# Attention output products one stretch earlier, and the column sums of w1 in f32r, in a fused attention and mixer kernel

## The chip, the cores and the metric

The kernel runs on one core of a Trainium2 chip. The metric is the device time of one execution in microseconds. The engines named here are PE (matrix products, with PEld for the loading of their weights), DVE and ACT (element-wise work; ACT does the exponentials), POOL (element-wise work on SBUF) and SP (here only a queue that issues DMAs).

## The reference

x is 2048 x 448. There are 16 heads of 28 columns that share one key and one value head. The outputs of attention and of a small mixer are weighed by a gate:

```python
q = (x @ wq).reshape(B, S, H, Dh).transpose(0, 2, 1, 3)
k = x @ wk
v = x @ wv
p = softmax(einsum("bhqd,bkd->bhqk", q, k) * Dh ** -0.5)
a = einsum("bhqk,bkd->bhqd", p, v).transpose(0, 2, 1, 3).reshape(B, S, H * Dh) @ wo
h = gelu(layernorm(x) @ w1)
x1 = x + concatenate(shifts of h's four column groups) @ w2
b = x1 + gelu(layernorm(x1) @ w3) @ w4
g = sigmoid((x * gate_w).sum(-1))
out = g * a + (1 - g) * b
```

## The kernel before

**Precision.** Most products are made in f32r: an operand is split into a high part (rounded to f32r) and a low part (what is left), and two or three products of the parts are added in PSUM. The products of values and of wo are plain f32.

**Stage 1 (to about 120 us).** Queries, keys, values and the gate are made by `stage_q`, four groups of heads for each of four blocks of 512 tokens, and go through DRAM. Between them stand the statistics of the first layer norm, and w1 is centred so that the norm's mean need not be subtracted: `sum_w1` adds the four row chunks of w1 on POOL to wsum, `centre_w1` sums wsum over the partitions by a product with a matrix of ones (line 396), and DVE subtracts the mean from w1. Then come the products with w1 and w2.

**Stage 2 (to about 400 us).** The products with w3 and w4, block by block.

**Stage 3 (to the end).** Attention in 16 units u, four blocks of 512 queries times four groups of four heads. A unit has 8 stretches v of two tiles of 128 keys; k = 8u + v counts the stretches. In a stretch stand, in this order:

- the scores of two key tiles (line 909): for each tile 12 products on PE into four banks, one for each head. The four heads use four row groups of PE side by side.
- for each tile, ACT's exponentials of heads 0, 1 and 2 from PSUM into p (line 942), and DVE's copy of head 3 into pd (line 939). There are 8 banks of PSUM, taken in turn by scores, products and values, and given back to the end of the row by whoever read them out. ACT makes the exponentials of both copies of pd at the end (line 947).
- in k = 3 to 10 one of eight late products with w4 (`w4_half`).
- from unit 1 on one half of an output product (`wo_half`, line 823): 128 tokens of an earlier unit by 224 columns of wo, evicted by DVE to ot (line 814). A unit has 8 halves, i = 0 to 7. In the last unit, two stand in each of the stretches 4 to 6, and two in the tail behind the loop.
- the values of the stretch before (line 952), in two halves of 256 queries, on four column groups of PE; DVE adds each half to o (line 956; a copy, line 967, where a unit begins).

The row sums of the softmax come out of the values' products as a column of ones. A unit is normalised in the next unit: in stretch 0 SP sends the sums as rt (`sums_begin`, line 789); in stretch 1 DVE checks them and makes reciprocals (`recip`, lines 785 and 796), and SP sends these to DRAM (rd, line 798) and back to all partitions (rb, line 800); in stretch 3 DVE multiplies o by rb to on (`norm`, line 805), which the half products of that unit read.

Every engine works through its instructions in the order in which the program lists them. For the attention loop that is the text of the loop.

Of the kernel before, what the change touches and what calls it, by code (L numbers as in the profile page):

```python
# [9 lines left out]
F32 = mybir.dt.float32  # L10
F32R = mybir.dt.float32r
AF = mybir.ActivationFunctionType
ALU = mybir.AluOpType
# [3 lines left out]
P = 128  # L17
S = 2048
D = 448
# [18 lines left out]
def f32(ap):  # L38
    return ap.bitcast(F32)
# [3 lines left out]
def gated_mix_kernel(  # L43
# [12 lines left out]
    nc = tc.nc  # L56
# [31 lines left out]
    def misc_tile(name):  # L88
        return psA.tile([P, 512], F32, tag="misc", bufs=1, name=name)
# [103 lines left out]
    NU = NB * NG  # L193
# [56 lines left out]
    with tc.tile_pool(name="s1b", bufs=1) as s1b, \  # L250
            tc.tile_pool(name="ps1", bufs=1, space=PSUM) as ps1:
        s1_stack = ExitStack()
        s1 = s1_stack.enter_context(tc.tile_pool(name="s1", bufs=1))
# [128 lines left out]
            rb_of[b] = s1.tile([P, 512], F32, tag="rsb", bufs=2, name=f"rsb_{b}")  # L382
            nc.sync.dma_start(rb_of[b][0:C], rd.rearrange("(o t) p -> o (t p)", o=1).broadcast_to([C, 512]))

        ones = s1.tile([P, P], F32, name="ones")
        nc.gpsimd.memset(ones, 1.0)
        wsum = s1.tile([P, 512], F32, tag="hf", bufs=3, name="wsum")[:, 0:D]

        def sum_w1():
            nc.gpsimd.tensor_tensor(wsum, w1raw[:, 0, :], w1raw[:, 1, :], ALU.add)  # L390
            nc.gpsimd.tensor_tensor(wsum, wsum, w1raw[:, 2, :], ALU.add)
            nc.gpsimd.tensor_tensor(wsum[0:64], wsum[0:64], w1raw[0:64, 3, :], ALU.add)

        def centre_w1():
            ps = misc_tile("wsum_ps")[:, 0:D]
            nc.tensor.matmul(ps, ones, wsum, start=True, stop=True)
            for c in range(4):
                nc.vector.scalar_tensor_tensor(w1raw[:, c, :], ps, -1.0 / D, w1raw[:, c, :],
                                               op0=ALU.mult, op1=ALU.add)
# [237 lines left out]
    with tc.tile_pool(name="s2", bufs=1, reuse_waits="tile") as s2, \  # L637
# [42 lines left out]
        for b in range(NB):  # L680
            acc = [ps2.tile([P, 512], F32, tag="acc", bufs=4, name=f"acc_{b}_{t}") for t in range(4)]
            gs = {}
            for f in range(NF):
# [35 lines left out]
                u = M_AT.get(b * NF + f)  # L719
# [32 lines left out]
    with tc.tile_pool(name="s3", bufs=1, reuse_waits="tile") as s3, \  # L752
# [7 lines left out]
        def take():  # L760
            return banks.pop(0)

        def bank(name):
            ps = banks.pop(0)
            banks.append(ps)
            return ps

        def q_fetch(u):
            if u < NU:
                q_load(u, s3.tile([P, 512], F32, tag="qr", bufs=1, name=f"qr_{u}"))  # L770

        def q_begin(u):
            q_split(u, s3.tile([P, 512], F32R, tag="qh", bufs=3, name=f"qh_{u}"),
                    s3.tile([P, 512], F32R, tag="ql", bufs=3, name=f"ql_{u}"), nc.gpsimd)
# [12 lines left out]
        def sums_begin(u, o):  # L787
            rt = s3.tile([P, 16], F32, tag="rt", bufs=2, name=f"rt_{u}")
            nc.sync.dma_start(rt, o[0:128:32, :].rearrange("j (a b) -> j a b", b=16))
            return u, o, rt  # L790
# [12 lines left out]
        def norm(u, o, rb):  # L803
            on_of[u] = s3.tile([P, 512], F32, tag="on", bufs=2, name=f"on_{u}")
            nc.vector.tensor_mul(on_of[u], o, rb)
# [11 lines left out]
        def wo_job(u, t, cols=slice(0, D), evict=by_one, queue=nc.sync, then=None):  # L817
            b, g = divmod(u, NG)
            n = 4 * b + t
            ps = take()  # L820
            for j in range(4):
                tok = slice(t * P + 32 * j, t * P + 32 * j + 32)
                nc.tensor.matmul(ps[32 * j:32 * j + 32, cols], on_of[u][:, tok], wof[:, g, cols],  # L823
                                 start=True, stop=True, tile_position=(0, 32 * j))
            if g == 0 and cols.start == 0:
                ot_of[n] = s3.tile([P, D], F32, tag="ot", bufs=5, name=f"ot_{n}")
            before = x1[:, n, cols] if g == 0 else ot_of[n][:, cols]
            def finish():
                evict(n, ps, before, cols)
                if g == NG - 1 and cols.stop == D:  # L830
                    queue.dma_start(out[0, n * P:(n + 1) * P, :], ot_of[n])
                banks.append(ps)

            if then is None:
                finish()
            else:
                then.append(finish)

        def wo_half(u, i, then=None):
            t, h = divmod(i, 2)  # L840
            wo_job(u, t, slice(224 * h, 224 * h + 224), then=then)
# [3 lines left out]
        def w4_half(i):  # L845
            t, h = divmod(i, 2)
            n = NT - 4 + t
            cols = slice(224 * h, 224 * h + 224)
            tok = slice(t * P, (t + 1) * P)
            gh, gl = last_g  # L850
            ps = bank(f"job_{n}_{h}")[:, cols]
            nc.tensor.matmul(ps, gh[:, tok], w4h[-1][:, 1, cols], start=True, stop=False)
            nc.tensor.matmul(ps, gh[:, tok], w4l[-1][:, 1, cols], start=False, stop=False)
            nc.tensor.matmul(ps, gl[:, tok], w4h[-1][:, 1, cols], start=False, stop=True)
            nc.vector.scalar_tensor_tensor(x1[:, n, cols], ps, gi[:, n:n + 1], x1[:, n, cols],
                                           op0=ALU.mult, op1=ALU.add)
# [44 lines left out]
        p_of, pd_of, o_of, sums, norms = {}, {}, {}, [], []  # L901
        NV = 8

        def scores(u, kt):
            bs = [take() for j in range(4)]
            for i in range(3):
                for j in range(4):
                    for _, _, w, a in score(u, bs[j], j, slice(kt * P, (kt + 1) * P), i=i):
                        nc.tensor.matmul(bs[j], w, a, start=(i == 0), stop=(i == 2), tile_position=(32 * j, 0))  # L909
            return bs  # L910
# [21 lines left out]
        def exps(u, kt, bs):  # L932
            ps = p_of[u, kt] = {}
            for j in READ:
                if j == DRAIN:
                    if kt % 2 == 0:
                        pd_of[u, kt // 2] = turn_of(pd_free)
                    ps[j] = pd_of[u, kt // 2][:, kt % 2, :]
                    nc.vector.tensor_copy(ps[j], bs[j])  # L939
                else:  # L940
                    ps[j] = turn_of(p_free)
                    behind[kt % 2] = nc.scalar.activation(ps[j], bs[j], AF.Exp, scale=SCALE)  # L942
                banks.append(bs[j])

        def late_exps(u, v):
            pd = pd_of.pop((u, v))
            ins = nc.scalar.activation(pd, pd, AF.Exp, scale=SCALE)  # L947
            tc.add_manual_dep(ins.ins, behind[0].ins.name, SYNC, reason="one wait of ACT for its own writes per stretch")

        def value(u, kt, q, pv):  # L950
            for j in range(4):
                nc.tensor.matmul(pv[32 * j:32 * j + 32, q], vext[:, kt, :], p_of[u, kt][j][:, q],  # L952
                                 start=(kt % 2 == 0), stop=(kt % 2 == 1), tile_position=(0, 32 * j))

        def add_value(u, q, pv):
            nc.vector.tensor_add(o_of[u][:, q], o_of[u][:, q], pv[:, q])  # L956
            banks.append(pv)

        def values(u, v):
            if v == 0:  # L960
                o_of[u] = s3.tile([P, 512], F32, tag="o", bufs=2, name=f"o_{u}")
            for q in HALVES:
                pv = take()
                for kt in (2 * v, 2 * v + 1):
                    value(u, kt, q, pv)
                if v == 0:
                    nc.vector.tensor_copy(o_of[u][:, q], pv[:, q])
                    banks.append(pv)
                else:
                    add_value(u, q, pv)  # L970
# [5 lines left out]
        W4_AT = 3  # L976

        for k in range(NU * NV - 1):
            u, v = divmod(k, NV)
            if k == 3:  # L980
                q_begin(1)
                q_fetch(2)
            if v == 6 and u + 2 < NU:
                q_begin(u + 2)
                q_fetch(u + 3)
            for kt in (2 * v, 2 * v + 1):
                exps(u, kt, scores(u, kt))
            late_exps(u, v)
            if 0 <= k - W4_AT < 8:
                w4_half(k - W4_AT)  # L990
            if v >= 4 and u:
                wo_half(u - 1, v - 4)
            if v < 4 and u > 1:
                wo_half(u - 2, v + 4)
            if v >= 4 and u == NU - 1:
                wo_half(u - 1, v)
            if k:
                values(*divmod(k - 1, NV))
            if u and v == 0:
                sums.append(sums_begin(u - 1, o_of[u - 1]))  # L1000
            if u and v == 1:
                norms.append(recip(*sums.pop()))
            if u and v == 3:
                norm(*norms.pop())
        assert not sums and not norms

        u, v = NU - 1, NV - 1
# [37 lines left out]
            value(u, NT - 2, q, pvs[i])  # L1045
        value(u, NT - 1, HALVES[0], pvs[0])
        add_value(u, HALVES[0], pvs[0])
        wo_half(u - 1, 3)
        later = []
        wo_half(u - 1, 7, later)  # L1050
        held = [tail_sums(0)]
# [80 lines left out]
```

## Time and profile before

| | |
|---|---|
| median of 3 runs | 918.75 us (917.4 to 918.87) |
| the profiled execution's own time | 918.12 us |
| its span, first to last instruction | 916.2 us |
| busy in it: PE, ACT, DVE, POOL | 907.5, 634.6, 542.8, 105.3 us |
| exponentials of ACT from PSUM, line 942 | 762, mean 619 ns |
| half products, line 823 | 992 instructions, mean 370 ns |
| products of values, line 952 | 4096 instructions, mean 379 ns |
| granted clock of PE | 0.999 |

A row of a timeline gives the start, the duration, the engine, line and operation, what is written and read, and how many instructions were merged. In brackets stands how long the engine was idle before it, and what ended that. Durations of PE overlap, since the next product enters while the last drains: the distance of two starts is what a product costs. An instruction of DVE may be shown to start shortly before the last one ends.

### The profile page before, as it was taken

The page shows a single profiled execution, that of the slowest core. Times are in us where ns is not written, and L with a number is a line of the kernel's source. Part 1 is how long each engine was busy: PE and PEld are TensorE (multiplying, and loading weights), DVE is VectorE, ACT ScalarE, POOL GpSimd, SP SyncE. Part 2 cuts the span into 40 slices and gives each one's busy share as a digit, 9 for nine tenths or more (in the row PEclk, how much of TensorE's full clock was granted, in tenths as well). Part 3 has the DMA queues.
Part 4 walks back from the last instruction along what each step waited for, and adds up shares of the span by engine and source line. Part 5 has one row for each costly group of instructions (what it writes and reads, how often), then busy time and mean ns, then how long its engine had stood idle before and what let it go on. Part 6 is the DMA issues. An engine that isn't in the chain of part 4 may idle for free.

```text
span 916.2 us, 24001 instructions
## 1 busy us (share of the span) xinstructions
PE 907.5 (99%) x10040; PEld 644.0 (70%) x10040; DVE 542.8 (59%) x1082; ACT 634.6 (69%) x1135; POOL 105.3 (11%) x136
## 2 busy tenths in 40 slices
PE   9999999999999999999999999999999999999997
PEld 7788888888888888875655565556656565556653
DVE  4674264631435736446666666676666666666765
ACT  5542255322232231259999999999999999999995
POOL 2243200212000430031000000000000000000000
PEclk9999999999999999999999999999999999999999
DMA  9822543220222132110000001100011000010001
GB/s 303 306 63 45 163 137 125 39 67 21 41 61 58 24 100 62 38 53 25 25 23 6 27 14 49 32 26 26 3 45 47 26 3 26 22 50 12 15 14 44
DMA packets 41809, 51.81 MB, mean 57 GB/s; under 512 B 9313, under 2 KB 27553, under 8 KB 41697
## 3 DMA queue, kind: packets, MB, share of 16 engines
q1 hardware_dynamic: 38528, 44.54, 16.5%
q10 hardware_dynamic: 3168, 5.70, 1.8%
q8 instruction: 80, 1.31, 0.6%
q14 instruction: 33, 0.26, 0.1%
HBM read 37.04 MB, written 11.93 MB: 53 GB/s over the span
## 4 chain that ended last, share of the span: by engine, by line
PE 97%; ACT 1%; DMA 0%; DVE 0%; issue 0%; ACTq 0%; DVEq 0%
PE bank L952 24%; PE bank L909 22%; PE bank L823 7%; PE acc L677 5%; PE acc L676 5%; PE acc L678 5%; PE g L132 4%; PE g L131 4%; PE g L133 4%; PE hs L455 1%; PE hs L456 1%; PE g L135 1%; PE g L134 1%; PE h L131 1%; PE h L132 1%; PE h L133 1%
## 5 line engine op out<-in xcount | busy, mean ns | idle before, releaser
L942 ACT ACTIVATE p<-bank 128x512 f32<-128x512 f32 x762 | 387.1, 619 | 4.4 <-PE bank L909 3.9
L952 PE MATMUL bank<-p,vext 128*32 128x256 f32 x3080 | 243.9, 379 | 0.8 <-ACT p L942 0.8
L952 PE MATMUL bank<-pd,vext 128*32 128x256 f32 x1016 | 240.3, 379 | 0.0
L939 DVE COPY pd<-bank 128x512 f32<-128x512 f32 x254 | 175.2, 691 | 52.8 <-PE bank L909 51.8
L952 PEld LDWEIGHTS bank<-p,vext 128*32 128x32 f32 x3080 | 125.1, 110 | 83.1 <-ACT p L942 2.1
L666 ACT ACTIVATE gh<-g 128x512 fp32r<-128x512 f32 x55 | 32.8, 597 | 187.4 <-PE g L135 187.4
L956 DVE TENSOR_TENSOR o<-o,bank 128x256 f32<-128x256 f32 x224 | 94.3, 421 | 94.5 <-ACT p L942 50.0
L947 ACT ACTIVATE pd<-pd 128x1024 f32<-128x1024 f32 x127 | 141.1, 1111 | 0.0
L909 PE MATMUL bank<-qh,kH 30*128 30x512 f32 x1024 | 119.0, 443 | 0.0
L668 DVE TENSOR_TENSOR gl<-gf,gh 128x512 fp32r<-128x512 f32 x55 | 37.9, 689 | 124.6 <-ACT gf L667 124.5
L952 PEld LDWEIGHTS bank<-pd,vext 128*32 128x32 f32 x1016 | 110.7, 110 | 0.0
L909 PE MATMUL bank<-ql,kH 28*128 28x512 f32 x1024 | 104.7, 390 | 0.0
L909 PE MATMUL bank<-qh,kL 28*128 28x512 f32 x1024 | 104.5, 391 | 0.0
L909 PEld LDWEIGHTS bank<-qh,kH 30*128 30x128 f32 x1024 | 60.8, 182 | 58.2 <-ACT p L942 47.0
L677 PE MATMUL acc<-w4l,gh 128*128 128x448 f32 x220 | 80.4, 366 | 0.0
L676 PE MATMUL acc<-w4h,gh 128*128 128x448 f32 x220 | 80.3, 365 | 0.0
L678 PE MATMUL acc<-w4h,gl 128*128 128x448 f32 x220 | 80.2, 364 | 0.0
L823 PE MATMUL bank<-wof,on 128*32 128x224 f32 (+1 forms) x992 | 72.9, 370 | 0.3 <-ACT p L942 0.3
L132 PE MATMUL g<-al,w3h 128*128 128x512 f32 x168 | 65.8, 392 | 0.0
L131 PE MATMUL g<-ah,w3h 128*128 128x512 f32 x168 | 65.6, 391 | 0.0
L133 PE MATMUL g<-ah,w3l 128*128 128x512 f32 x168 | 65.5, 390 | 0.0
L909 PEld LDWEIGHTS bank<-ql,kH 28*128 28x128 f32 x1024 | 51.6, 185 | 9.0
(193 smaller groups left out, 1164.1 us busy)
## 6 DMA issues: line engine op xcount, KB each, us to landing
qd<-qf ACTq DMA_DIRECT2D x16, 256.0 KB
qm<-qd SPq DMA_DIRECT2D x16, 256.0 KB
qr<-qd SPq DMA_DIRECT2D x16, 256.0 KB
rb<-rd SPq DMA_DIRECT2D x15, 256.0 KB
x<-in_x_dram SPq DMA_DIRECT2D x4, 896.0 KB
xd<-xt SPq DMA_DIRECT2D x16, 224.0 KB
w34raw<-in_w_dram SPq DMA_DIRECT2D x7, 512.0 KB
w34raw<-in_w_dram SPq DMA_DIRECT2D x7, 448.0 KB
```

What stands on the lines that cost most here:

```text
L131: nc.tensor.matmul(ps, wh[:, c, :], ah[:, c, :], start=(c == 0), stop=False)
L132: nc.tensor.matmul(ps, wh[:, c, :], al[:, c, :], start=False, stop=False)
L133: nc.tensor.matmul(ps, wl[:, c, :], ah[:, c, :], start=False, stop=False)
L676: nc.tensor.matmul(ps, gh[:, tok], w4h[i][:, k, :], start=(f == 0), stop=False)
L677: nc.tensor.matmul(ps, gh[:, tok], w4l[i][:, k, :], start=False, stop=False)
L678: nc.tensor.matmul(ps, gl[:, tok], w4h[i][:, k, :], start=False, stop=(f == stop))
L823: nc.tensor.matmul(ps[32 * j:32 * j + 32, cols], on_of[u][:, tok], wof[:, g, cols], start=True, stop=True, tile_position=(0, 32 * j))
L909: nc.tensor.matmul(bs[j], w, a, start=(i == 0), stop=(i == 2), tile_position=(32 * j, 0))
L939: nc.vector.tensor_copy(ps[j], bs[j])
L942: behind[kt % 2] = nc.scalar.activation(ps[j], bs[j], AF.Exp, scale=SCALE)
L947: ins = nc.scalar.activation(pd, pd, AF.Exp, scale=SCALE)
L952: nc.tensor.matmul(pv[32 * j:32 * j + 32, q], vext[:, kt, :], p_of[u, kt][j][:, q], start=(kt % 2 == 0), stop=(kt % 2 == 1), tile_position ...
```

## The change

In a stretch of the loop the reciprocals (stretch 1) and the normalisation (stretch 3) move ahead of the half products and values, directly behind the copies and exponentials. The half products of a unit move up by one stretch: i = 0 stands at the end of stretch 3, behind the values; i = 1 to 4 in stretches 4 to 7; i = 5 to 7 in stretches 0 to 2 of the next unit. In the last unit, unit 14's halves stand as 0 in stretch 3, (1, 2), (3, 4) and 5 in stretches 4 to 6, and 6 and 7 in the tail.

The sum of w1 is split by POOL into wsh and wsl, both f32r, and the product with ones becomes two f32r products.

```diff
-        ones = s1.tile([P, P], F32, name="ones")
-        nc.gpsimd.memset(ones, 1.0)
+        ones = s1.tile([P, P], F32R, name="ones")
+        nc.gpsimd.memset(f32(ones), 1.0)
         wsum = s1.tile([P, 512], F32, tag="hf", bufs=3, name="wsum")[:, 0:D]
+        wsh = s1.tile([P, 512], F32R, tag="hf", bufs=3, name="wsh")[:, 0:D]
+        wsl = s1.tile([P, 512], F32R, tag="hf", bufs=3, name="wsl")[:, 0:D]
 
         def sum_w1():
...
             nc.gpsimd.tensor_tensor(wsum[0:64], wsum[0:64], w1raw[0:64, 3, :], ALU.add)
+            nc.gpsimd.tensor_copy(wsh, wsum)
+            nc.gpsimd.tensor_tensor(wsl, wsum, f32(wsh), ALU.subtract)
 
         def centre_w1():
             ps = misc_tile("wsum_ps")[:, 0:D]
-            nc.tensor.matmul(ps, ones, wsum, start=True, stop=True)
+            nc.tensor.matmul(ps, ones, wsh, start=True, stop=False)
+            nc.tensor.matmul(ps, ones, wsl, start=False, stop=True)
...
             late_exps(u, v)
-            if 0 <= k - W4_AT < 8:
-                w4_half(k - W4_AT)
-            if v >= 4 and u:
-                wo_half(u - 1, v - 4)
-            if v < 4 and u > 1:
-                wo_half(u - 2, v + 4)
-            if v >= 4 and u == NU - 1:
-                wo_half(u - 1, v)
-            if k:
-                values(*divmod(k - 1, NV))
-            if u and v == 0:
-                sums.append(sums_begin(u - 1, o_of[u - 1]))
             if u and v == 1:
                 norms.append(recip(*sums.pop()))
             if u and v == 3:
                 norm(*norms.pop())
+            if 0 <= k - W4_AT < 8:
+                w4_half(k - W4_AT)
+            if v < 3 and u > 1:
+                wo_half(u - 2, v + 5)
+            if v > 3 and u:
+                for i in (v - 3,) if u < NU - 1 else ((1, 2), (3, 4), (5,))[v - 4]:
+                    wo_half(u - 1, i)
+            if k:
+                values(*divmod(k - 1, NV))
+            if v == 3 and u:
+                wo_half(u - 1, 0)
+            if u and v == 0:
+                sums.append(sums_begin(u - 1, o_of[u - 1]))
...
-        wo_half(u - 1, 3)
+        wo_half(u - 1, 6)
         later = []
         wo_half(u - 1, 7, later)
```

How the instructions of DVE stand in unit 1, stretch 1, before (the copies of head 3, a product of w4, the values into o, check and reciprocal):

```order
L939 COPY pd_3535<-bank_3506 128x512
L939 COPY pd_3535<-bank_3502 128x512
L855 SCALAR_TENSOR_TENSOR x_72<-bank_3503,gi,x_72 128x224
L967 COPY o_4058<-bank_3506 128x256
L967 COPY o_4058<-bank_3508 128x256
L785 SCALAR_TENSOR_TENSOR good<-rt_4019,good 128x16
L796 RECIPROCAL rr_4078<-rt_4019 128x16
```

The same stretch and stretch 3 in the changed kernel (the lines are 5 higher):

```order
L944 COPY pd_3540<-bank_3511 128x512
L944 COPY pd_3540<-bank_3507 128x512
L790 SCALAR_TENSOR_TENSOR good<-rt_4024,good 128x16
L801 RECIPROCAL rr_4060<-rt_4024 128x16
L860 SCALAR_TENSOR_TENSOR x_72<-bank_3508,gi,x_72 128x224
L972 COPY o_4070<-bank_3511 128x256
L972 COPY o_4070<-bank_3513 128x256
```

```order
L944 COPY pd_3542<-bank_3508 128x512
L944 COPY pd_3542<-bank_3512 128x512
L810 TENSOR_TENSOR on_4177<-o_3612,rb_4064 128x512
L961 TENSOR_TENSOR o_4070<-o_4070,bank_3507 128x256
L961 TENSOR_TENSOR o_4070<-o_4070,bank_3508 128x256
L819 SCALAR_TENSOR_TENSOR ot_4201<-bank_3510,gg,x_72 128x224
```

Check and reciprocal moved ahead of three evictions; the normalisation, which stood behind both additions of stretch 3, moved ahead of them, and a half product's eviction (L819) came to the end of that stretch.

PE at the end of that stretch 3 (k = 11), before: the last values are followed by the scores of stretch 4.

```order
L952 MATMUL bank_3503<-p_3527,vext 32x256
L952 MATMUL bank_3503<-p_3528,vext 32x256
L952 MATMUL bank_3503<-pd_3536,vext 32x256
L909 MATMUL bank_3505<-qh_3677,kH 128x512
L909 MATMUL bank_3508<-qh_3677,kH 128x512
```

In the changed kernel, the first half product (four products on column tiles) stands between them:

```order
L957 MATMUL bank_3508<-p_3532,vext 32x256
L957 MATMUL bank_3508<-p_3533,vext 32x256
L957 MATMUL bank_3508<-pd_3541,vext 32x256
L828 MATMUL bank_3510<-wof,on_4177 32x224 x4
L914 MATMUL bank_3513<-qh_3682,kH 128x512
L914 MATMUL bank_3511<-qh_3682,kH 128x512
```

Before, the first half product of unit 0 stood in stretch 4, ahead of its values.

## The prediction

> **What bounds the kernel now.** I read the page first (busy time of each engine, then the chain of work that ended last), then the timelines of PE, ACT, DVE and SP over a few stretches of the attention loop, then the DMA share in short windows.
>
> ```profile
> PE 907.5 (99%) x10040; PEld 644.0 (70%) x10040; DVE 542.8 (59%) x1082; ACT 634.6 (69%) x1135; POOL 105.3 (11%) x136
> PE 97%; ACT 1%; DMA 0%; DVE 0%; issue 0%; ACTq 0%; DVEq 0%
> ```
>
> PE is busy 907.5 of 916.2 us, and 97% of the chain is PE. So only a shorter PE program, or fewer waits in it, shortens the run. The attention loop fills the second half of the span; here is one of its stretches in the timeline of PE (start, duration):
>
> ```profile
> 564.11 0.51 PE L909 MATMUL bank<-qh,kH 30*128 30x512 f32 x4
> ...
> 565.76 0.59 PE L823 MATMUL bank<-wof,on 128*32 128x224 f32 x8
> 566.16 0.39 PE L952 MATMUL bank<-p,vext 128*32 128x256 f32 x3
> ...
> 567.67 0.39 PE L952 MATMUL bank<-p,vext 128*32 128x256 f32 x3
> ...
> 568.00 0.51 PE L909 MATMUL bank<-qh,kH 30*128 30x512 f32 x4
> ```
>
> Scores take 564.11 to 565.76 (1.65 us), one half of an output product 0.40, the values 566.16 to 568.00 (1.84): 3.89 us. The reader should see that nothing stands empty between them. ACT is close behind. At the head of the loop, where PE has less to do, ACT sets its own pace:
>
> ```profile
> 408.31 3.10 ACT L942 ACTIVATE p<-bank 128x512 f32<-128x512 f32 x6
> ...
> 412.12 3.16 ACT L942 ACTIVATE p<-bank 128x512 f32<-128x512 f32 x6
> ```
>
> That is 412.12 - 408.31 = 3.81 us a stretch. So a stretch costs the larger of PE's sum and 3.81: a stretch with one half product is PE's by 0.08 us, one with none is ACT's, and one with two is PE's alone. The rows of PE at the two ends of the loop show the other two kinds:
>
> ```profile
> 447.42 0.51 PE L909 MATMUL bank<-qh,kH 30*128 30x512 f32 x4
> ...
> 449.06 0.42 PE L952 MATMUL bank<-p,vext 128*32 128x256 f32 x3
> ...
> 450.92 0.50 PE L909 MATMUL bank<-qh,kH 30*128 30x512 f32 x4
> ...
> 452.93 0.59 PE L823 MATMUL bank<-wof,on 128*32 128x224 f32 x8 [0.32 <-ACT p L942]
> ...
> 455.18 0.51 PE L909 MATMUL bank<-qh,kH 30*128 30x512 f32 x4
> ```
>
> ```profile
> 895.53 0.51 PE L909 MATMUL bank<-qh,kH 30*128 30x512 f32 x4
> ...
> 897.17 0.96 PE L823 MATMUL bank<-wof,on 128*32 128x224 f32 x16
> ...
> 899.79 0.51 PE L909 MATMUL bank<-qh,kH 30*128 30x512 f32 x4
> ```
>
> The first set is stretch 3 of unit 1 (k = 11), the only one late in the loop with neither a half product nor a product of w4. PE passes it in 450.92 - 447.42 = 3.50 us, and in the next stretch it waits 0.32 us for ACT, so that one takes 4.26. The second set is stretch 6 of the last unit: two half products, 4.26 us, ACT waiting.
>
> **The change, part by part.**
>
> *Half products one stretch earlier.* A unit still has eight of them, one a stretch. What differs is the ends of the loop. The first now falls into k = 11, and the last unit's stretch 6 has one instead of two (the tail keeps two). k = 11 and 12 together took 455.18 - 447.42 = 7.76 us and will take 2 x 3.89 = 7.78: +0.02, since the free PE time there was lost again to ACT. Stretch 6 goes from 4.26 to 3.89: -0.37. Bounds: the new product in k = 11 costs at least nothing and at most its own 0.40; the one removed saves at least nothing and at most 0.40.
>
> *Stretch 3: the product behind the values.* In all 15 units from u = 1 on, scores are followed by values, and the product comes last. From the start of a stretch to the first group behind the scores it is 1.65 us where that is a product (565.76) and 1.64 where it is a value (449.06 - 447.42), so the entry costs the same. The exit from values to scores is 568.00 - 567.67 = 0.33 us, a group every (567.67 - 566.16)/7 = 0.216, so 0.11 is the change of kind; no row shows an exit from a product to scores. I bound it by 0.11 us less and 0.11 more per unit, 1.7 us each way over 15 units, and take nothing, since both are groups of four products on the same four column tiles.
>
> *Reciprocal behind the copies of stretch 1, normalisation behind those of stretch 3.* These are DVE instructions that can now hold up what is queued behind them: the eviction of the half product and the two additions of the values, and through them the banks of the next scores. DVE's rows of unit 5, stretches 1 and 3:
>
> ```profile
> 565.21 1.39 DVE L939 COPY pd<-bank 128x512 f32<-128x512 f32 x2 [0.49 <-PE bank L909]
> 566.51 0.44 DVE L814 SCALAR_TENSOR_TENSOR ot<-bank,gg,ot 128x224 f32<-128x224 f32 x1
> 567.28 0.42 DVE L967 COPY o<-bank 128x256 f32<-128x256 f32 x1 [0.32 <-PE bank L952]
> 568.21 0.42 DVE L967 COPY o<-bank 128x256 f32<-128x256 f32 x1 [0.51 <-ACT p L942]
> 568.55 0.17 DVE L785 SCALAR_TENSOR_TENSOR good<-rt,good 128x16 f32<-128x16 f32 x1
> ...
> 573.00 1.40 DVE L939 COPY pd<-bank 128x512 f32<-128x512 f32 x2 [0.49 <-PE bank L909]
> ...
> 575.06 0.42 DVE L956 TENSOR_TENSOR o<-o,bank 128x256 f32<-128x256 f32 x1 [0.31 <-PE bank L952]
> 575.98 0.42 DVE L956 TENSOR_TENSOR o<-o,bank 128x256 f32<-128x256 f32 x1 [0.50 <-ACT p L942]
> 576.32 0.68 DVE L805 TENSOR_TENSOR on<-o,rb 128x512 f32<-128x512 f32 x1
> ```
>
> and SP's, with the DMA share (the last column but one) while rt and rb move:
>
> ```profile
> 564.75 0.56 SPq L789 DMA_DIRECT2D rt<-o  x1
> 566.99 0.33 SPq L831 DMA_DIRECT2D out_dram<-ot  x1
> 568.90 0.33 SPq L798 DMA_DIRECT2D rd<-rr  x1
> 570.33 0.54 SPq L800 DMA_DIRECT2D rb<-rd  x1
> ```
>
> ```profile
> 566.00:566.30 0.30, 0.30 (x12) 0.23 (x8) 0.30 (x1) 0.30 (x2) 0.00 (x0) 1.00 0.20 23
> 566.30:566.50 0.20, 0.20 (x12) 0.12 (x4) 0.20 (x1) 0.20 (x1) 0.00 (x0) 1.00 0.00 0
> ...
> 573.80:574.40 0.60, 0.60 (x20) 0.37 (x15) 0.60 (x2) 0.60 (x3) 0.00 (x0) 1.00 0.24 92
> ```
>
> Is rt there in time? It is issued at 564.75. Its data are gone from the DMA engines by 566.30, and the check at 568.55 used it without a wait: it lands between these. The nearest landing that a row shows is rd, also 8 KB: the issue that waits for it starts 570.33 - 568.90 = 1.43 us after its own, which for rt gives 566.2, or 566.4 with its issue 0.23 us longer. DVE comes to the reciprocal at 565.21 + 1.39 = 566.60. I take no wait. Check and reciprocal hold DVE about 0.3 us (estimate: 0.17 and the same again), the eviction moves from 566.51 to 566.9, and the 0.32 us that DVE now idles before 567.28 takes nearly all of it; the addition at 568.21 is on time. Cost nothing, as long as rt lands by about 567.3: from landing to the release of the last bank are 0.3 + 0.44 + 0.42 + 0.42 = 1.6 us at most, and PE's second scores of the next stretch, which need it, begin near 568.8 (568.00 and half of the 1.65). Without that cover, at the upper bound of 568.55, it is 1.2 us a unit, 18 us in all.
>
> Is rb there in time? The reciprocal ends near 566.9, so rb, 1.43 us behind rd, is issued at 568.35 instead of 570.33. Its data still move at 574.40 at most 4.1 us after the issue, and the normalisation took it unwaited at 576.32, 6.0 after: it lands between 572.4 and 574.35. The copies of stretch 3 end at 573.00 + 1.40 = 574.40. So even the late bound hides it. The normalisation then runs to about 575.1. Without the product ahead of them the values start 0.40 us earlier, so the first addition is due at 574.66 and waits 0.4 us; the second is due at 575.58 and is on time. The product starts at 573.54 + 1.73 = 575.27 at the earliest (573.54 is 571.89 + 1.65, and 571.89 is 564.11 + 2 x 3.89): 0.2 us behind the normalisation that it needs. Its eviction then ends near 576.4, where before the second addition ended (575.98 + 0.42), so the last bank comes free when it did. Cost nothing.
>
> [...]
>
> SP's order changes with it: rd and rb now stand ahead of the store that was at 566.99. In the units 5, 9 and 13 a store now goes out in stretch 0, at the same place of the stretch, so near 566.99 - 3.89 = 563.1, 1.65 us ahead of rt. If it delays rt, that is rival 1 in three units only: 0.9 us at its 0.3 a unit.
>
> *Column sums of w1.* PE's rows in the first stage, and POOL's:
>
> ```profile
> 23.11 0.39 PE L135 MATMUL q<-ahk,wql 128*128 128x512 f32 x1
> 23.34 0.91 PE L396 MATMUL wsum_ps<-wsum,ones 128*128 128x448 f32 x2
> 23.74 0.75 PE L131 MATMUL q<-ahk,wqh 128*128 128x512 f32 x1
> 24.33 0.40 PE L132 MATMUL q<-alk,wqh 128*128 128x512 f32 x1
> ```
>
> ```profile
> 17.85 1.15 POOL L392 TENSOR_TENSOR wsum<-wsum,w1raw 64x448 f32<-64x448 f32 x1
> 26.77 0.20 POOL L143 TENSOR_TENSOR rs_s<-mv_s,epst 128x4 f32<-128x4 f32 x1 [7.78 <-DVE mv_s L140]
> ```
>
> ```profile
> L185 POOL TENSOR_TENSOR ql<-qr,qh 128x512 fp32r<-128x512 f32 x15 | 19.3, 1286 | 1.2
> ```
>
> A product of 512 columns in f32r is followed by the next after 23.34 - 23.11 = 0.23 us. From the f32 sum at 23.34 to the second product behind it are 0.99 us, of which 0.23 is that of one f32r product: the sum takes 0.76. Two f32r products of 448 columns take 2 x 0.23 x 448/512 = 0.40. Saved: 0.36 us (bounds 0 and 0.76). POOL has a cast and a subtraction more: at most 2 x 1.29 us from L185, ending by 19.0 + 2.6 = 21.6, ahead of the 23.34 where PE needs them and of POOL's next work at 26.77. Cost nothing; without that cover at most 1.7 us, once. PE has work without pause behind it, so the 0.36 should reach the end.
>
> *Sum:* 0.02 - 0.37 - 0.36 = -0.71 us. Span 916.2 to 915.5, that execution's 918.12 to 917.4. The median of the runs, 918.75, lies 0.63 above that execution, so I predict **918.0 us**, with an own range of 917.2 to 919.0.
>
> **Rivals.**
>
> 1. *rt is late (slower).* It lands after 567.3 and DVE stands with three evictions queued behind it; PE then waits for banks in stretch 2. For it: the upper bound of 568.55, and that DVE asks only 0.2 us after rt is expected. Against: its data are off the engines by 566.30. At 567.6 it is 0.3 us x 15 = 4.5, or 922.5; at the bound 936.
> 2. *rb is late or the exit from the product costs (slower side).* PE stands at the product of stretch 3, or 0.11 us are added there: 15 x 0.11 = 1.7, or 919.7. For it: only 0.2 us lie between normalisation and product. Against: the bounds of rb.
> 3. *The exit from the product is cheaper, or the evictions fall better (faster).* 0.11 to 0.15 us a unit: 918.0 - 2 = 916.0. For it: a group of a product has 224 columns, that of a value 256. Against: PE's group rate in the loop is even.
> 4. *The savings don't arrive.* The 0.36 of w1 is swallowed by a later wait, or the tail takes back that of stretch 6: 918.75.
>
> **How the numbers follow.** Forecast 0.73, rival 1 0.09, rival 2 0.07, rival 3 0.07, rival 4 0.04. What a measurement of this kernel can tell from no change is about 0.2%, or 1.8 us; the runs of before spread over 1.5. Faster than 916.9: rival 3 and 0.05 of the forecast's spread, 0.12. Slower than 920.6: rival 1 and 0.02 of rival 2's upper part, 0.11. The rest, 0.77, is no change that can be told. The range from 916.4 to 920.4 holds the forecast, rival 4 and most of rivals 2 and 3.
>
> **What would show it.** Right, if the profile after has: the two products of the sum 0.40 us together; starts of scores 3.89 us apart from unit 1 on, stretches 1 and 3 included; k = 11 and 12 both at 3.89; the last unit's stretch 6 at 3.89 and its stretches 4 and 5 still at about 4.27; no idle time of DVE ahead of the check put down to the DMA of rt, none ahead of the normalisation. Wrong, if stretch 1 or 2 grows in each unit (rt), if PE waits for "on" at the product of stretch 3 (rb), or if stretch 3 alone is shorter or longer by a tenth of a microsecond (the exit).

## The result, and the profile after

The changed kernel takes 920.51 us (median of 20 runs, 918.0 to 922.49), the kernel before 918.14 beside it (20 runs, 916.93 to 919.07): a ratio of 1.0027, interval 1.002 to 1.0033. It is slower by 0.27%, where 918.0 us and no change that can be told were forecast. The profiled execution took 921.01 us, its span 919.1 against 916.2.

Both parts that were to save time did so at their own places. First PE around the column sums of w1 in the profile after (start, duration):

```profile
23.64 0.39 PE L135 MATMUL q<-ahk,wql 128*128 128x512 f32 x1
23.87 0.36 PE L400 MATMUL wsum_ps<-wsh,ones 128*128 128x448 f32 x1
24.07 0.37 PE L401 MATMUL wsum_ps<-wsl,ones 128*128 128x448 f32 x1
24.28 0.39 PE L131 MATMUL q<-ahk,wqh 128*128 128x512 f32 x1
```

From the first of the two products to the one behind them are 24.28 - 23.87 = 0.41 us, where the f32 sum took 0.76; POOL's subtraction for it is done at 19.91 + 1.16 = 21.07:

```profile
19.91 1.16 POOL L396 TENSOR_TENSOR wsl<-wsum,wsh 128x448 fp32r<-128x448 f32 x1
```

Then the scores' first products at k = 11 and 12, and in the last unit's stretch 6 and behind it:

```profile
448.54 0.50 PE L914 MATMUL bank<-qh,kH 30*128 30x512 f32 x4
...
452.43 0.51 PE L914 MATMUL bank<-qh,kH 30*128 30x512 f32 x4
...
899.22 0.51 PE L914 MATMUL bank<-qh,kH 30*128 30x512 f32 x4
...
903.10 0.50 PE L914 MATMUL bank<-qh,kH 30*128 30x512 f32 x4
```

3.89 and 3.88 us. What was lost lies in the waits of DVE and of SP's queue (us in total, times, longest), after:

```profile
DVE on L810 <- DMA rb<-rd: 2.2, 7, 0.7
DVE o L961 <- ACT p L947: 43.1, 85, 0.9
DVE good L790 <- DMA rt<-o: 0.4, 1, 0.4
...
SPq L805 <- DMA rd<-rr: 28.3, 15, 2.3
```

and before:

```profile
DVE o L956 <- ACT p L942: 50.0, 101, 0.5
SPq L800 <- DMA rd<-rr: 16.4, 15, 1.5
```

The normalisation waits for rb in 7 of 15 units, where before it waited in none. The queue waits 28.3/15 = 1.9 us for rd before it can issue rb, instead of 1.1. And the longest wait in front of an addition is 0.9 instead of 0.5 us. These are two separate losses; each has its place in the loop.

**Loss 1: rb.** Unit 8 is the worst, k = 64 to 71. SP's rows, and the DMA of the window in which rd is under way (662.07 to 664.3):

```profile
659.85 0.56 SPq L794 DMA_DIRECT2D rt<-o  x1
662.07 0.31 SPq L803 DMA_DIRECT2D rd<-rr  x1
664.28 0.54 SPq L805 DMA_DIRECT2D rb<-rd  x1
```

```profile
q1 hardware_dynamic: 144, 0.01, 4.2%
q8 instruction: 1, 0.02, 2.8%
```

rd now takes 664.28 - 662.07 = 2.21 us instead of 1.4, and in that time one of the 16 DMA engines carries one packet that is not data: a fetch of instructions, 16 KB, 2.8% of 16 engines over 2.23 us = 1.0 us long. In the trace 15 of rd's 16 parts have landed 1.4 us after the issue (so in 14 of the 15 units), the last one 0.8 us later in this unit. The trace does not say which DMA engine carries a part, but it ties the late one to the fetch: in 14 of the 15 units the last part lands 1.03 to 1.08 us behind the end of PE's fetch, at whatever distance the two began (in unit 3, which an 8 KB fetch meets as well, 1.14). DVE and PE in stretch 3 of unit 8:

```profile
668.08 1.39 DVE L944 COPY pd<-bank 128x512 f32<-128x512 f32 x2 [0.49 <-PE bank L914]
670.18 0.69 DVE L810 TENSOR_TENSOR on<-o,rb 128x512 f32<-128x512 f32 x1 [0.71 <-DMA rb<-rd]
670.79 0.75 DVE L961 TENSOR_TENSOR o<-o,bank 128x256 f32<-128x256 f32 x2
```

```profile
666.97 0.51 PE L914 MATMUL bank<-qh,kH 30*128 30x512 f32 x4
...
670.18 0.38 PE L957 MATMUL bank<-pd,vext 128*32 128x256 f32 x1
671.02 0.58 PE L828 MATMUL bank<-wof,on 128*32 128x224 f32 x8 [0.45 <-ACT p L947]
671.53 0.51 PE L914 MATMUL bank<-qh,kH 30*128 30x512 f32 x4
```

The copies end at 669.47, rb is there at 670.18, the normalisation ends at 670.87 and PE's product starts at 671.02. The row puts the wait of PE down to ACT, which had long been done; it is "on" that came last. The stretch takes 671.53 - 666.97 = 4.56 us. Over the loop stretch 3 exceeds 3.89 in seven units: k = 19, 43, 67, 75, 107, 115 and 123 by 0.28, 0.11, 0.67, 0.23, 0.19, 0.23 and 0.14, in sum **1.85 us**.

**Loss 2: DVE.** Three stretches that have no normalisation take 4.16 us as well: k = 57, 88 and 119, exactly 31 apart. PE's first scores of k = 57 and 58, then DVE's two additions and the next copy at k = 57:

```profile
627.82 0.51 PE L914 MATMUL bank<-qh,kH 30*128 30x512 f32 x4
...
631.98 0.50 PE L914 MATMUL bank<-qh,kH 30*128 30x512 f32 x4
```

```profile
627.09 0.42 DVE L961 TENSOR_TENSOR o<-o,bank 128x256 f32<-128x256 f32 x1 [0.32 <-PE bank L957]
628.36 0.42 DVE L961 TENSOR_TENSOR o<-o,bank 128x256 f32<-128x256 f32 x1 [0.85 <-ACT p L947]
628.91 0.69 DVE L944 COPY pd<-bank 128x512 f32<-128x512 f32 x1
```

The second addition stands 0.85 us instead of 0.50, though by PE's timeline the last value had ended at 627.89, as early as in other stretches. It frees the last bank of the next scores, and PE loses 0.27: three times, **0.81 us**.

**What differs in the clock.** The two profiled executions are 2.9 us apart; a part of it belongs to neither kernel. The windows from the head of the loop, after (the last columns are the granted clock, DMA share and GB/s), and the value products of that stretch in its chain of waits, with a later one:

```profile
403.30:408.40 5.10, 5.10 (x49) 3.06 (x48) 2.92 (x5) 3.99 (x8) 4.72 (x5) 1.00 0.70 229
408.40:412.20 3.80, 3.34 (x33) 1.38 (x32) 1.12 (x2) 3.80 (x7) 1.39 (x2) 0.55 0.03 9
```

```profile
408.94 3.47 PE bank L957 x32
...
418.46 1.86 PE bank L957 x32
```

For 3.4 us PE had half its clock, which the profiled execution of before had not at this place. Of the 26 runs of before beside the first experiments, though, the 3 with a mean granted clock of 0.997 took 919.22 us on average, the 11 with 1.0 took 917.63. In the fourteen profiles of this document every execution with a mean of 0.997 has this half clock and none with 0.999 or more has it (with 0.998 some do), so it very likely meets that kernel too. At equal mean clock the changed kernel took 921.08 (5 runs) and 919.67 (5 runs), 1.9 and 2.0 us more. The two losses and the three small terms give 1.85 + 0.81 - 0.38 - 0.35 + 0.02 = 1.95. That agrees, but it does not show each term: the loop's first scores start at 403.41 us after and 403.49 before, so only 0.08 of the 0.35 is seen there, and over the fourteen profiles this start lies anywhere from 402.5 to 403.8.

### The profile page after: what moved, and what is told of

It is laid out like the page before. It is cut to its first block, busy times and chain, and to the rows that moved or that the text cites. A ratio compares the mean times of both kernels' runs of the same rounds, so it can differ in the third digit from the quotient of the medians.

```text
span 919.1 us, 24002 instructions
## 1 busy us (share of the span) xinstructions
PE 911.5 (99%) x10040; PEld 645.0 (70%) x10040; DVE 544.4 (59%) x1082; ACT 635.4 (69%) x1135; POOL 107.3 (12%) x138
## 4 chain that ended last, share of the span: by engine, by line
PE 98%; ACT 1%; DVE 0%; issue 0%; DVEq 0%; ACTq 0%
PE bank L957 24%; PE bank L914 22%; PE bank L828 7%; PE acc L682 5%; PE acc L681 5%; PE acc L683 5%; PE g L132 4%; PE g L131 4%; PE g L133 4%; PE hs L460 1%; PE hs L461 1%; PE g L135 1%; PE g L134 1%; PE h L131 1%; PE h L132 1%; PE h L133 1%
```

## The experiments

Times are medians; "before" is the kernel before, run beside them on the same chip. The ratio is not the quotient of the two medians, and differs from it by up to 0.0007, or 0.6 us.

**The two parts apart.** The kernel before with the two products of w1, and the changed kernel with the old sum.

> The kernel before with the column sums of w1 by two f32r products, the loop untouched. My theory: 0.36 us less than before in the median (span 915.8 against 916.2), the sum at 0.41 us instead of 0.76, the loop at its old 496.3 us, stretch 3 of every unit at 3.89. Rival: the half clock seen at the loop's start of the changed kernel comes from this part; then the granted clock is 0.997 in many runs and the time is 0.5 to 1 us above before.

> The changed kernel with the column sums of w1 as they were, so the loop's change alone. My theory: the loss is the loop's, so 0.36 us above the changed kernel's 920.5, about 2.7 us above before; the normalisation waits 0.2 to 0.7 us for the DMA of rb in about half of the units, and three stretches of 4.16 us 31 stretches apart stay. Rival (w1 is to blame for the half clock): about 1 us less than the changed kernel, and a granted clock of 1.0 in all runs.

w1 alone: 917.95 us against 918.15, ratio 1.0 (0.9991 to 1.0009): too small to be told. The loop alone: 920.42, ratio 1.0026 (1.0016 to 1.0035), with no half clock in its profiled execution and the three stretches of 4.16 in it. Loss 1 is smaller in this execution: stretch 3 exceeds 3.89 by 0.39, 0.08, 0.20 and 0.24, in sum 0.9. So the loss is the loop's, and the size of loss 1 changes from execution to execution. The half clock isn't w1's: the runs of w1 alone had clocks from 0.997 to 1.0, and it shows below in a profile without the w1 part.

**Early normalisation without a product behind it.**

```diff
             late_exps(u, v)
+            if u and v == 1:
+                norms.append(recip(*sums.pop()))
+            if u and v == 3:
+                norm(*norms.pop())
             if 0 <= k - W4_AT < 8:
...
-            if u and v == 1:
-                norms.append(recip(*sums.pop()))
-            if u and v == 3:
-                norm(*norms.pop())
```

> The kernel before with reciprocal and normalisation behind the copies of their stretches, and every half product where it was before (none needs the normalisation in its own stretch). My theory: rd to rb is 1.6 to 2.65 us as in the changed kernel and the normalisation waits for rb in some units, but PE now feels it only through the banks that the two additions behind it release: at most 0.5 us in all, time within 0.5 us of before. Rival (the product behind the values costs PE 0.1 us per exit, rb nothing): exactly before's time, and all of the loss in the next kernel. Second rival (DVE's later additions alone are the loss): 1.5 us or more above before.

919.78 us, ratio 1.0011 (1.0002 to 1.002). That is more than the 0.5 us I allowed. The waits for rd, and one stretch 3 of DVE:

```profile
SPq L800 <- DMA rd<-rr: 31.1, 15, 2.4
```

```profile
701.40 0.69 DVE L805 TENSOR_TENSOR on<-o,rb 128x512 f32<-128x512 f32 x1 [0.83 <-DMA rb<-rd]
702.01 0.45 DVE L814 SCALAR_TENSOR_TENSOR ot<-bank,gg,ot 128x224 f32<-128x224 f32 x1
702.37 0.74 DVE L956 TENSOR_TENSOR o<-o,bank 128x256 f32<-128x256 f32 x2
```

rd is as late as in the changed kernel, and a late normalisation now holds up an eviction and two additions. The stretch behind it, 4, grew in four units by 0.37, 0.12, 0.44 and 0.19, in sum 1.1 us, through the banks alone. So the product behind the values isn't needed for the loss; it only feels it sooner. This execution had the half clock, with w1 as before.

**Normalising in two pieces.** In the first version the 128 columns that product 0 reads come between the two additions, in the second behind the copies; the other 384 behind that product's eviction in both. The edit shown is the second version; `norm` takes the columns as an argument.

```diff
             if u and v == 3:
-                norm(*norms.pop())
+                norm(*norms[-1], slice(0, P))
...
             if v == 3 and u:
                 wo_half(u - 1, 0)
+                norm(*norms.pop(), slice(P, 512))
```

> The changed kernel, but in stretch 3 only the 128 columns that the first half product reads are normalised, between the two additions of the values, and the other 384 behind that product's eviction. My theory: rb has 0.7 to 1 us more to land, so 1.3 to 1.85 us less than the changed kernel, about 918.8 to 919.2; stretch 3 is 3.89 in all but one or two units. Rival (the exit from a product to scores costs PE): no gain, 920.5 or slightly more for the added instruction.

> The changed kernel, but behind the copies of stretch 3 only the 128 columns that the first half product reads are normalised, and the other 384 behind that product's eviction. My theory: the normalisation in front of the product is 0.4 us shorter, so each loss of a unit shrinks by 0.4 (0.28, 0.11, 0.67, 0.23, 0.19, 0.23, 0.14 leave 0.27 in sum): 1.6 us less than the changed kernel, 918.9. If it is the exit from the product, or the product's place as such, that costs: no gain. Between the additions, the same split cost 0.24 us in every unit, since the product then stood 0.2 us behind it.

The first took 923.23 us, 1.0055 (1.0041 to 1.0069), the worst of all. No wait for rb is left in it, yet stretch 3 takes 4.08 to 4.26 in every unit, 4.13 in most. DVE and PE there:

```profile
577.59 0.42 DVE L962 TENSOR_TENSOR o<-o,bank 128x256 f32<-128x256 f32 x1 [0.35 <-PE bank L958]
577.92 0.29 DVE L811 TENSOR_TENSOR on<-o,rb 128x128 f32<-128x128 f32 x1
```

```profile
577.93 0.39 PE L958 MATMUL bank<-p,vext 128*32 128x256 f32 x3
577.95 0.38 PE L958 MATMUL bank<-pd,vext 128*32 128x256 f32 x1
578.36 0.58 PE L829 MATMUL bank<-wof,on 128*32 128x224 f32 x8
```

The piece ends at 578.21, and PE, which would have come to the product a group behind 577.93, at 578.15, starts it at 578.36. I had traded a loss in half of the units for a sure one of 0.24 in all. The second version took 919.6, 1.0017 (1.0008 to 1.0026): 0.9 us less than the changed kernel, not 1.6. Its losses to rb are down to 0.13, 0.09 and 0.28, as expected in kind; it has two stretches of 4.16 left, and the rest of the difference I can't place.

**Moving PE's instruction fetches.** PE fetches 16 KB every two stretches, which is 256 of its instructions (a stretch has 64 products and 64 weight loads). Since 128 instructions make one stretch, the fetch comes at the same place of each unit: in the trace after it begins 2.0 to 2.9 us behind the issue of rt in all 15 units, and rd is issued 2.2 to 2.6 behind it. Before, the fetch is there too (2.2 to 2.8), but rd goes out at 4.15.

```diff
-    for _ in range(20):
-        nc.tensor.matmul(wps[:, 0:256], warm[:, 0:P], warm, start=True, stop=True)
+    for _ in range(84):
+        nc.tensor.matmul(wps[:, 0:60], warm[:, 0:P], warm[:, 0:60], start=True, stop=True)
```

> The changed kernel with 84 warm-up products of 60 columns in place of 20 of 256, about the same 4.4 us ahead of the first real product but 128 more PE instructions, so that PE's 16 KB instruction fetches come 3.9 us earlier, at 1.7 us ahead of rt instead of 2.2 us behind it, where rd is under way. My theory: rd lands in 1.4 us in every unit, rb is issued 3.6 to 3.8 us behind rt instead of 4.0 to 4.9, the normalisation waits nowhere, stretch 3 is 3.89 in every unit: 1.85 us less than the changed kernel, 918.7. Rival (rd is late because it shares a DMA engine or the memory with something else, as q or an output store): rd stays at 2.0 to 2.65 us and the time at 920.5.

> The kernel before with the warm-up of 84 short products, its loop untouched: a control for the warm-up. My theory: no change (within 0.3 us of before), since there rd goes out behind the fetch anyway, and rb has 0.5 us to spare. Rival (the warm-up itself, or another place of PE's fetches, shortens the run): 1 us or more below before, and then the gain in the changed kernel wasn't rd's.

The changed kernel with that warm-up: 918.21 us against 917.82, ratio 0.9998 (0.9989 to 1.0006), which is 2.3 us less than without it. Its waits and one unit of SP:

```profile
SPq L805 <- DMA rd<-rr: 16.2, 15, 1.8
```

```profile
784.01 0.56 SPq L794 DMA_DIRECT2D rt<-o  x1
786.24 0.32 SPq L803 DMA_DIRECT2D rd<-rr  x1
787.64 0.54 SPq L805 DMA_DIRECT2D rb<-rd  x1
```

rd to rb is 1.40 to 1.46 us in 14 of 15 units. The fifteenth kept a loss (stretch 3 of 4.32, rd 2.15 us), and the DMA of its window, 505.4 to 507.6, says why: an 8 KB fetch of another queue had met it.

```profile
q14 instruction: 1, 0.01, 1.1%
```

The kernel before with the same warm-up: 917.78 against 918.07, ratio 1.0001 (0.9992 to 1.001). The warm-up by itself gives nothing that can be told, so the gain is rd's. Its size is less sure than its cause: 2.3 us by the medians, 2.0 if each kernel is compared with the runs of before beside it, and 1.85 - 0.43 = 1.4 by stretch 3 in the two traces.

**Moving DVE's fetches.** In four units DVE runs 264 instructions, its semaphores counted, 66 a unit; 8 KB are 128 of them, at 64 bytes as PE's are, or 15.5 stretches. Memsets ahead of the loop move that boundary: four on a new tile of 4 bytes a partition, alone and with the warm-up, then two and four on a tile that was there.

```diff
+        pad = s3.tile([P, 1], F32, name="pad")
+        for i in range(4):
+            nc.vector.memset(pad, 1.0)
         for k in range(NU * NV - 1):
```

> The changed kernel with four tiny memsets on VectorE ahead of the loop, so that the 8 KB instruction fetch of DVE falls four instructions earlier in its program. My theory: the three stretches of 4.16 us, 31 apart, are a stall of DVE at that fetch in front of a late addition; they go (the stall falls where DVE idles), 0.8 us less than the changed kernel, 919.7. Rival (they are bank waits of the new order): they stay at 4.16 and the time stays at 920.5.

> The changed kernel with the warm-up of 84 short products and the four memsets. My theory: both losses go, 2.65 us less than the changed kernel, 917.9 or a little less, 0.3 to 0.7 us below before, as the prediction had it. If either shift only moves the collision (rb in place of rd, another addition in place of this one), it stays above 919.

Four alone: 921.25 us (6 runs), 1.004 (1.0026 to 1.0054). Four with the warm-up: 918.58, 1.0008 (0.9999 to 1.0017). Both miss. In both the three long stretches left k = 57, 88 and 119 and appeared at 41, 72 and 103, half a period of 31 away: four instructions are half a stretch, and every second boundary had lain half a stretch off. The trace lets one count: with all records of DVE numbered from zero, semaphores included, the additions that stand are 959, 1215 and 1471 in the changed kernel and 831, 1087 and 1343 in these two. In all eight profiles that have such stretches, the number is 63 above a multiple of 128. So the place is shown; what holds DVE there is not. The 8 KB fetch next to it starts at 629.06 in the changed kernel, 0.7 us after the addition of 628.36 had started, so the addition did not wait for that transfer. And in both the scores took 1656 instead of 1644 ns in the median, start of scores to first half product: 1.3 us over the 110 stretches from k = 12 on.

> As the run with both shifts, but the four memsets write a tile that is there already. There every stretch was about 0.007 us longer, its scores 1656 ns instead of 1644 from first score to first product. Theory: the 4-byte tile moved the query tiles to another address, and the products of the scores were slower for it; here the scores take 1644 again, the three stretches of 4.16 at the same places (41, 72, 103) stay, and the time is 0.7 us less than there, about 918.0. Rival (DVE's memsets or the fetch phase made the scores longer): 1656 again.

> The changed kernel with the two memsets alone. My theory: the three stretches of 4.16 go, the losses to rb stay: 0.8 us less than the changed kernel, about 1.2 us above before. Rival (the three stretches are not DVE's fetch): no gain.

With four memsets on an old tile and the warm-up: 918.2, 1.0005 (0.9997 to 1.0014); the scores take 1644 ns again (the twelve profiles without the new tile lie between 1644 and 1649), so the 12 ns came with the new tile and not with the memsets. That it moves what is allocated behind it may be the reason; this was not tried apart. The long stretches are still at 41, 72 and 103, the first of them in DVE's rows:

```profile
564.00 0.42 DVE L961 TENSOR_TENSOR o<-o,bank 128x256 f32<-128x256 f32 x1 [0.85 <-ACT p L947]
```

With two alone: 920.41, 1.0027 (1.0016 to 1.0038). The long stretches are gone from its profile, as expected, but the time isn't lower: stretch 3 lost 0.38, 0.28, 0.48, 0.75 and 0.54 to rb there, 2.4 us instead of 1.85. The places of the stretches bear the theory out, the time of this run does not show it.

> The changed kernel with the warm-up of 84 short products and two memsets on a tile that is there already (no new address behind it). DVE fetches 128 instructions every 15.5 stretches, so the four memsets of the run before only brought the fetches between the old ones in front of an addition; two bring neither there. My theory: no stretch of 4.16, none lost to rb, 0.8 us less than with the warm-up alone: 0.5 to 0.8 us below before, 917.2 to 917.5. Rival (any shift meets an addition somewhere): three stretches of 4.16 again, at another place, and the time at before's.

Two memsets with the warm-up, the only run meant to be without either loss: **917.41 us against 918.07**, ratio 0.9993 (0.9984 to 1.0002). The mean of its 11 runs is 917.36, that of the 35 of before 918.10: 0.74 less, the size of the forecast's 0.71, though the interval doesn't exclude no change. It had the half clock in its profiled execution. Its waits:

```profile
DVE o L961 <- ACT p L947: 43.1, 87, 0.5
...
SPq L805 <- DMA rd<-rr: 16.4, 15, 1.9
```

No wait for rb is left, and the longest in front of an addition is 0.5 again. From k = 11 on all stretches are 3.88 to 3.90 except the last unit's 4 and 5. The way from k = 11 to the last scores is 451.78 us in this trace and 452.37 before: 0.59 less, where the loop's part of the forecast was 0.35. The rest is about 2 ns in every stretch, which no run explains.

## Why the prediction was wrong

- *Half products one stretch earlier, and w1:* as predicted at their places. k = 11 and 12 at 3.89, stretch 6 of the last unit at 3.88, its stretches 4 and 5 at 4.27; the sum of w1 0.41 us for the 0.40 taken. POOL was done 2.8 us ahead of PE. That the saving of w1 reaches the end of the run is not shown: alone it gave 917.95 us against 918.15, within its interval.
- *The exit from the product:* as predicted, nothing. Stretch 3 of a unit without a wait, in the run with both shifts (first products of the scores, last group of values, product, next scores):

```profile
697.14 0.51 PE L914 MATMUL bank<-qh,kH 30*128 30x512 f32 x4
...
700.32 0.39 PE L957 MATMUL bank<-p,vext 128*32 128x256 f32 x3
700.54 0.56 PE L828 MATMUL bank<-wof,on 128*32 128x224 f32 x8
701.03 0.50 PE L914 MATMUL bank<-qh,kH 30*128 30x512 f32 x4
```

  The values pass into the product at their own pace (0.22), the product and its exit take 0.49, that is 0.40 and the 0.09 to 0.11 that the exit from the values had cost: 3.89.
- *rt:* as predicted but for one wait. DVE's check waited for it once in 15 units, 0.4 us, and stretch 1 grew nowhere.
- *rb:* here the prediction failed, at "rb, 1.43 us behind rd, is issued at 568.35 instead of 570.33" and so at "even the late bound hides it". The 1.43 was read from one unit, in which rd went out at 4.15 us behind rt. Moved to 2.2, it met PE's instruction fetch, and rd to rb became 1.66 to 2.71 us; rb was issued 4.0 to 4.9 us behind rt where 3.60 was taken. The kernel before had shown that the row is not fixed: in two of its 15 units, 1 and 3, an 8 KB fetch met rd, and rd to rb took 1.86 and 1.82 us. Unit 1:

```profile
444.29 0.32 SPq L798 DMA_DIRECT2D rd<-rr  x1
446.15 0.58 SPq L800 DMA_DIRECT2D rb<-rd  x1
```

  The bounds of rb's own transfer held. The working left 0.2 us between normalisation and product, so a term late by up to 1.3 us had nothing to hide it. Rival 2 had the place, and was given 0.07. That its 919.7 came near is luck: the 1.7 us were the price of an exit that cost nothing, and it put the danger in rb itself, not in rd.
- *DVE's second addition:* no step of the prediction spoke of it. Which instruction has the place 63 above a multiple of 128 changes with their order. Before, from number 703 to 1471, these are copies, a semaphore and first additions, and PE lost nothing there; after, three of them are second additions, which free the last bank for PE: 0.81 us.
- *The forecast's sum* agrees with the run without either loss, -0.74 us for -0.71, but its interval (about -1.5 to +0.2 us) is too wide to show it.

## What to carry to other kernels

A DMA that is moved meets other traffic than the row its duration was read from: look in the DMA rows of the new time slot, instruction fetches among them, before the old duration is carried over, above all where the margin is 0.2 us. Read the duration in every round of the loop, too, and not in one. Where a round holds whole fetches, as here (1024 PE instructions a unit, 256 a fetch), such a meeting repeats in every round, and a few instructions ahead of the loop move it. A change of order that is right in its sum can be lost to such phases, so read every single stretch, not the mean.

## What the hardware showed

- An instruction fetch is DMA traffic: one packet of 16 KB for PE, 0.9 to 1.4 us long, every two stretches. A transfer of 8 KB in 16 parts that it met had its last part 1.64 to 2.65 us after the issue instead of 1.4, and (in 14 of 15 units) 1.03 to 1.08 us after the fetch's end.
- Where an addition had a number 63 above a multiple of 128 among DVE's records, DVE stood 0.85 us ahead of it instead of 0.50, so 0.35 us with its input ready by PE's timeline.
- A tile of 4 bytes a partition, allocated ahead of others, made the scores 12 ns slower in each stretch. Which tile's address did it was not tried.
- PE's granted clock was halved for 3.4 us at the head of the loop in the profiled executions of seven kernels, the changed one among them, and not in those of seven others; the single runs' mean clocks suggest that it meets before as well.
